# A decode attention kernel with less instruction code: register loops in place of written-out code on TensorE and VectorE

## The chip, the cores and the metric

One core of a Trainium2 chip runs the whole program. The metric is device time in microseconds (us), the median of several executions. Each comparison below ran both kernels on the same chip. "Fast" is the normal state of a run.

The engines are named as in the profile: PE is TensorE (PEld its weight loads), DVE VectorE, ACT ScalarE, POOL GpSimd, SP SyncE. Times without another word are microseconds from the start of the span.

## The reference, cut to what matters

Four tokens (B = 4, D = 512) pass through attention over a sliding window of a cache, and in parallel through a SwiGLU block.

```python
def reference(A_x, A_k_cache, A_v_cache, A_wq, A_wo, B_x, B_w_gate, B_w_up, B_w_down):
    x = A_x                                   # (4, 1, 512) bf16
    xn = _layernorm(x, axis=-1)               # eps 1e-5
    # attention: 32 query heads, 8 K/V heads, Dh 128, the last W = 4096 of 16384 positions
    q = (xn @ wq) ...                         # wq 512 x 4096
    scores = einsum("bhqd,bhkd->bhqk", q, k) * Dh ** -0.5
    o = softmax(scores) @ v
    att = o.reshape(B, 1, 4096) @ wo          # wo 4096 x 512
    ffn = (silu(xn @ w_gate) * (xn @ w_up)) @ w_down      # F = 1792
    return x + att + ffn
```

There are 32 pairs of a token and a K/V head. Each pair needs 1 MB of K and 1 MB of V, that is 67 million bytes of cache in all and 14 million of weights, 81.0 MB as the profile counts it.

## The kernel before

SyncE issues every load in one queue, in order. A load waits only where its buffer is still in use. Four slots each hold K and V.

```python
@block.sync
def _(eng):
    def load_k(i):
        if i >= NSL:                                   # NSL = 4
            eng.wait_ge(s_tr, NG * (i - NSL + 1))      # transposes of pair i-4 done
        eng.dma_start(KB[i % NSL][:], kv_ap(A_k_cache, i)).then_inc(d_k[i % NSL], 16)
    def load_v(i):
        if i == NSL - 1:
            eng.wait_ge(s_pv, 1)                       # the fourth V waits for the first P.V
        if i >= NSL:
            eng.wait_ge(s_pv, i - NSL + 2)
        eng.dma_start(VB[i % NSL][:], kv_ap(A_v_cache, i)).then_inc(d_v[i % NSL], 16)
    # W_Q half, X, W_Q half, K0, W_gate, W_up, W_down, V0, then K1 V1 ... K31 V31, then 8 loads of W_O
```

The slot of the fourth V holds zeros at first. P·V is the product of a pair's softmax weights P with its V. The first P·V is a dummy that multiplies them, so that the loop over pairs needs no special first pass. Therefore **no load after K3 is issued until TensorE has done its prologue and that first P·V**.

TensorE's prologue is written out, one matmul per line of the unrolled loop:

```python
for c in range(NC):                                    # Q: 4 x 32 matmuls
    if c % 2 == 0:
        eng.wait_ge(d_wq[c // 2], 16)
    for h in range(HQ):
        last = mm(q_ps[:, h * B:(h + 1) * B], WQ[:, c, h * Dh:(h + 1) * Dh], XnT[:, c, :], ...)
last.then_inc(s_q, 1)
for w, d, o in ((WG, d_wg, gate_ps), (WU, d_wu, up_ps)):   # gate, up: 14 x 4 matmuls each
    eng.wait_ge(d, 16)
    ...
# [cut: 14 down matmuls]
eng.wait_ge(s_nrm, 1)
with eng.Fori(0, HKV) as r:                            # the main loop was already a register loop
    for b in range(B):
        transposes(r, b)      # 32 transposes of K into PSUM, VectorE copies them out
        pv(r, b)              # P.V of the pair before
        scores(r, b)          # 32 matmuls, then exp on ScalarE
# [cut: permutation and W_O]
```

VectorE's code for the 32 pairs is written out, `for i in range(NPAIR): evac(i); ...; norm(i - 1)`.

The softmax here doesn't subtract the row's maximum and nothing guards it: scores larger than these inputs give would overflow.

## Time and profile before

| | before |
|---|---|
| time, median (lowest to highest) | 202.88 us (202.8 to 203.15), 3 runs |
| span of the profiled run | 201.1 us |
| bytes read | 81.01 MB at 403 GB/s over the span |
| PE busy | 80% |
| fourth V issued (= first P·V done) | 38.19 us |
| last W_O landing | 197.79 us |

The page of the kernel before: the slices are fortieths of the span (5.03 us), with busy tenths of PE and of the 16 DMA engines and the bandwidth, and then the chain that ended last, that is the waits followed back from the last instruction.

```profile
span 201.1 us, 7838 instructions
...
PE   0043779989989779797999889797979799795992
...
DMA  6999999999999999999999999999999999999980
GB/s 218 431 429 425 428 420 417 419 419 420 420 417 417 422 429 419 420 422 419 429 422 419 424 416 425 425 417 422 420 425 425 419 419 420 425 424 407 410 328 8
...
DMA 58%; PE 27%; DVE 6%; SPq 5%; issue 2%; ACT 0%; DVEq 0%
DMA kbuf<-in_A_k_cache_dram 39%; PE ps_kt L321 15%; DMA wu_sb<-in_B_w_up_dram 11%; DMA wo_sb<-in_A_wo_dram 9%; DVE kT L239 5%; PE ps_s L327 4%; PE ps_o L338 4%; SPq L174 3%; PE ps_m L311 2%; PE ps_m L303 2%; SPq L171 1%; PE ps_o L336 0%; PE ps_acc L352 0%; SPq L164 0%; SPq L180 0%
```

Reading it: DMA is at 9 from the second to the 38th of the 40 slices, at about 420 GB/s. PE is also nearly full, but the chain gives it 27% and DMA 58%. The queue of loads is never empty, so the stream of bytes decides the time.

TensorE's prologue and the issue of the loads that follow, from the timeline (start, duration, engine, line, operation, and in brackets the idle time before and what ended it):

```profile
13.47 3.57 PE L295 MATMUL ps_acc<-xnT,wq_sb 128*128 128x4 bf16 x128 [0.27 <-DVE xnT L227]
21.26 3.52 PE L303 MATMUL ps_m<-xnT,wg_sb 128*128 128x4 bf16 x56 [4.21 <-DMA wg_sb<-in_B_w_gate_dram]
25.39 3.52 PE L303 MATMUL ps_m<-xnT,wu_sb 128*128 128x4 bf16 x56 [0.61 <-DMA wu_sb<-in_B_w_up_dram]
```

```profile
38.19 0.33 SPq L171 DMA_DIRECT2D vbuf<-in_A_v_cache_dram  x1
38.56 0.43 SPq L164 DMA_DIRECT2D kbuf<-in_A_k_cache_dram  x1
```

128 Q matmuls take 3.57 us, and gate and up 3.52 us each. PE waits 4.21 us for W_gate in between. Written-out matmuls follow each other every 28 ns on average (3.57 us / 128); the weights arrive later than PE can use them. The up projection ends at 28.9 us and the fourth V is issued at 38.19 us, while earlier loads are still in flight until about 43 us.

Instruction fetches appear in the trace's DMA records as packets of their own. PE's are of 16384 B, at 19.1, 29.6, 42.4, 48.7, 55.3 and 194.6 us. The other engines' are of 8192 B, at 56.5, 117.5, 182.4 and 183.4 us. The records name a queue (q8 and q14) and not an engine; whose they are is inferred.

### The profile page before, as it was taken

The page shows a single profiled execution, that of the slowest core. Times are in us where ns is not written, and L with a number is a line of the kernel's source. Part 1 is how long each engine was busy: PE and PEld are TensorE (multiplying, and loading weights), DVE is VectorE, ACT ScalarE, POOL GpSimd, SP SyncE. Part 2 cuts the span into 40 slices and gives each one's busy share as a digit, 9 for nine tenths or more (in the row PEclk, how much of TensorE's full clock was granted, in tenths as well). Part 3 has the DMA queues.
Part 4 walks back from the last instruction along what each step waited for, and adds up shares of the span by engine and source line. Part 5 has one row for each costly group of instructions (what it writes and reads, how often), then busy time and mean ns, then how long its engine had stood idle before and what let it go on. Part 6 is the DMA issues. An engine that isn't in the chain of part 4 may idle for free.

```text
span 201.1 us, 7838 instructions
## 1 busy us (share of the span) xinstructions
PE 160.3 (80%) x3539; PEld 151.5 (75%) x3539; DVE 112.0 (56%) x277; ACT 11.9 (6%) x36; POOL 7.2 (4%) x29
## 2 busy tenths in 40 slices
PE   0043779989989779797999889797979799795992
PEld 0043662879989779797999889797979799795971
DVE  0340010686786666676666657576767657574640
ACT  2020000000000000000000000000000000000000
POOL 8600000000000000000000000000000000000000
PEclk9999999997999997969556957879797958788555
DMA  6999999999999999999999999999999999999980
GB/s 218 431 429 425 428 420 417 419 419 420 420 417 417 422 429 419 420 422 419 429 422 419 424 416 425 425 417 422 420 425 425 419 419 420 425 424 407 410 328 8
DMA packets 11138, 81.15 MB, mean 404 GB/s; under 512 B 1268, under 2 KB 1272, under 8 KB 2296
## 3 DMA queue, kind: packets, MB, share of 16 engines
q1 hardware_dynamic: 11112, 81.01, 97.1%
q8 instruction: 6, 0.10, 0.2%
q14 instruction: 4, 0.03, 0.0%
q10 hardware_dynamic: 16, 0.00, 0.0%
HBM read 81.01 MB, written 0.00 MB: 403 GB/s over the span
## 4 chain that ended last, share of the span: by engine, by line
DMA 58%; PE 27%; DVE 6%; SPq 5%; issue 2%; ACT 0%; DVEq 0%
DMA kbuf<-in_A_k_cache_dram 39%; PE ps_kt L321 15%; DMA wu_sb<-in_B_w_up_dram 11%; DMA wo_sb<-in_A_wo_dram 9%; DVE kT L239 5%; PE ps_s L327 4%; PE ps_o L338 4%; SPq L174 3%; PE ps_m L311 2%; PE ps_m L303 2%; SPq L171 1%; PE ps_o L336 0%; PE ps_acc L352 0%; SPq L164 0%; SPq L180 0%
## 5 line engine op out<-in xcount | busy, mean ns | idle before, releaser
L239 DVE COPY kT<-ps_kt 128x1024 bf16<-128x1024 bf16 x128 | 83.2, 687 | 47.7 <-PE ps_kt L321 47.3
L321 PE MATMUL ps_kt<-ident,kbuf 128*128 128x128 bf16 x1024 | 82.7, 255 | 10.7 <-DMA kbuf<-in_A_k_cache_dram 10.2
L321 PEld LDWEIGHTS ps_kt<-ident,kbuf 128*128 128x128 bf16 x1024 | 76.4, 117 | 12.9 <-issue 10.2
L327 PE MATMUL ps_s<-qC,kT 128*128 128x4 bf16 x1024 | 30.8, 165 | 6.5 <-DVE kT L239 6.4
L327 PEld LDWEIGHTS ps_s<-qC,kT 128*128 128x128 bf16 x1024 | 28.1, 97 | 8.2 <-DVE kT L239 8.1
L338 PE MATMUL ps_o<-p,vbuf 128*128 128x4 bf16 x1056 | 32.2, 165 | 0.0
L338 PEld LDWEIGHTS ps_o<-p,vbuf 128*128 128x128 bf16 x1056 | 31.5, 99 | 0.0
L202 ACT ACTIVATE p<-ps_s 128x128 bf16<-128x128 f32 x32 | 8.9, 278 | 152.9 <-PE ps_s L327 152.9
L287 PE MATMUL ps_m<-i,xn 4*128 4x4 f32 x4 | 0.6, 254 | 12.6 <-DVE xn L225 12.6
L287 PEld LDWEIGHTS ps_m<-i,xn 4*128 4x128 f32 x4 | 0.5, 207 | 12.6 <-issue 12.6
L245 DVE TENSOR_REDUCE den<-ps_o 128x4 f32<-128x128 f32 x32 | 9.1, 284 | 0.9 <-PE ps_o L338 0.8
L336 PE MATMUL ps_o<-p,ones 128*128 128x128 bf16 x33 | 8.3, 250 | 0.0
L247 DVE RECIPROCAL den<-den 128x4 f32<-128x4 f32 x32 | 5.7, 178 | 2.7 <-issue 0.4
L249 DVE TENSOR_TENSOR oT<-ps_o,den 128x4 bf16<-128x4 f32 x32 | 5.4, 168 | 2.7 <-issue 0.4
L303 PE MATMUL ps_m<-xnT,wg_sb 128*128 128x4 bf16 x56 | 3.5, 199 | 4.2 <-DMA wg_sb<-in_B_w_gate_dram 4.2
L303 PEld LDWEIGHTS ps_m<-xnT,wg_sb 128*128 128x128 bf16 x56 | 3.4, 159 | 4.3 <-DMA wg_sb<-in_B_w_gate_dram 4.3
L253 DVE TENSOR_SCALAR ex<-ex 128x56 f32<-128x56 f32 x1 | 0.2, 192 | 11.6 <-ACT ex L199 11.6
L311 PE MATMUL ps_m<-wd_sb,guT 128*4 128x512 bf16 x14 | 4.8, 518 | 1.7 <-DVE guT L259 1.7
L244 DVE COPY qC<-qT 128x4 bf16<-128x4 bf16 x28 | 4.6, 163 | 2.6 <-PE ps_o L338 2.3
L211 DVE TENSOR_REDUCE st_sum<-x_sb 4x1 f32<-4x512 bf16 x1 | 0.7, 673 | 8.3 <-DMA x_sb<-in_A_x_dram 8.3
L352 PE MATMUL ps_acc<-wo_sb,oP 128*4 128x128 bf16 x128 | 4.1, 306 | 1.3 <-DMA wo_sb<-in_A_wo_dram 1.3
L311 PEld LDWEIGHTS ps_m<-wd_sb,guT 128*4 128x4 bf16 x14 | 1.4, 107 | 4.7 <-issue 2.4
(44 smaller groups left out, 40.8 us busy)
## 6 DMA issues: line engine op xcount, KB each, us to landing
kbuf<-in_A_k_cache_dram SPq DMA_DIRECT2D x32, 1024.0 KB, 15.5
vbuf<-in_A_v_cache_dram SPq DMA_DIRECT2D x32, 1024.0 KB, 13.3
wq_sb<-in_A_wq_dram SPq DMA_DIRECT2D x2, 2048.0 KB, 9.5
wo_sb<-in_A_wo_dram SPq DMA_DIRECT2D x8, 512.0 KB, 18.3
wg_sb<-in_B_w_gate_dram SPq DMA_DIRECT2D x1, 1792.0 KB, 18.6
wu_sb<-in_B_w_up_dram SPq DMA_DIRECT2D x1, 1792.0 KB, 22.2
wd_sb<-in_B_w_down_dram SPq DMA_DIRECT2D x1, 1792.0 KB, 26.0
out_dram<-y_sb SPq DMA_DIRECT2D x2, 1.0 KB
```

What stands on the lines that cost most here:

```text
L174: eng.dma_start(WO[:, q], wo_ap[q]).then_inc(d_wo[q], 16)
L202: eng.activation(P[j % 2][:], ps_S[:, 0:NT * REP].rearrange("p (t h) -> p t h", h=REP), ACT.Exp, scale=SCALE).then_inc(s_p, 1)
L239: eng.tensor_copy(KT[i % 2][:, a:a + 8, :], kt_ps[g % 4]).then_inc(s_ev, 1)
L245: eng.tensor_reduce(den[:], den_ps.rearrange("p (t h) -> p h t", h=REP), AX.X, ALU.add)
L247: eng.reciprocal(den[:], den[:])
L249: eng.tensor_tensor(OT[:, j // B, :, j % B], O_ps, den[:], ALU.mult).then_inc(s_nrm, 1)
L303: last = mm(o[:, t * B:(t + 1) * B], w[:].rearrange("p c (m t) -> p c t m", t=NF)[:, c, t, :], XnT[:, c, :], start=(w is WG and t == 0 and ...
L311: last = mm(down_ps, guT[:, t, :], WD[:, t, :], start=(t == 0), stop=(t == NF - 1))
L321: last = eng.transpose(kt_ps[n % 4][:, k, :], KB[b][:, 8 * g + k, :], ident[:])
L327: last = mm(ps_S[:, REP * t:REP * (t + 1)], KT[b % 2][:, t, :], QC[:, b])
L336: mm(den_ps, ones[:], P[p % 2][:].rearrange("p t h -> p (t h)"))
L338: last = mm(O_ps, VB[p][:, t, :], P[p % 2][:, t, :], start=(t == 0), stop=(t == NT - 1))
```

## The change

The intent is less instruction code, and so fewer instruction fetches on the DMA engines that carry the cache (in the trace of before, with a fetch of 16384 B at 19.1 us, 15 of W_gate's 16 landings come by 19.84 us and one at 21.21 us). TensorE's Q, gate and up become loops over registers (`Fori`: the engine itself counts in a register and branches back), VectorE's 32 pairs become a loop, there are 74 loads in place of 78, W_O uses two column tiles of 256 with two output DMAs, and the layernorm is shortened, with X loaded by ScalarE's queue. The score matmuls read Q at a register address in place of a copy by VectorE. The core of the diff (cuts marked with `...`):

```diff
-            for c in range(NC):
-                if c % 2 == 0:
-                    eng.wait_ge(d_wq[c // 2], 16)
-                for h in range(HQ):
-                    last = mm(q_ps[:, h * B:(h + 1) * B], WQ[:, c, h * Dh:(h + 1) * Dh], XnT[:, c, :], ...
+            zero = VB[:, (NSL - 1) * KVN:(NSL - 1) * KVN + 128]
+            mm(q_ps, zero, zero, start=True, stop=False, skip_group_check=True)
+            mm(ps_m[:, 0:128], zero, zero, start=True, stop=False, skip_group_check=True)
+            for g in range(2):
+                eng.wait_ge(d_wq[g], 16)
+                with eng.Fori(0, 8) as j:
+                    o = q_ps[:, ds((j & 3) * 32, 32)]
+                    w = WQf[:, ds(j * 1024 + 8192 * g, 1024)]
+                    x = XTf[:, ds((j & 4) + 8 * g, 4)]
+                    for k in range(8):
+                        last = mm(o[:, 4 * k:4 * k + 4], w[:, 128 * k:128 * k + 128], x, start=False, ...
...
             for w, d, o in ((WG, d_wg, 0), (WU, d_wu, 64)):
                 eng.wait_ge(d, 16)
-                for t in range(NF):
-                    for c in range(NC):
+                with eng.Fori(0, NF // 2) as t:
+                    oo = ps_m[:, ds(t * 8 + o, 8)]
+                    ww = w[:].rearrange("p c (m t) -> p c t m", t=NF)[:, :, ds(t * 2, 2), :]
+                    for k in range(2):
+                        for c in range(NC):
...
-            for i in range(NPAIR):
+            with eng.Fori(0, NPAIR) as i:
                 evac(i)
-                if i > 0:
-                    norm(i - 1)
+                norm(i)
...
-            eng.tensor_scalar(xc[:], X[:], st_mean[:, 0:1], None, ALU.subtract)
-            eng.tensor_tensor(xsq[:], xc[:], xc[:], ALU.mult)
-            eng.tensor_reduce(st_sum[:], xsq[:], AX.X, ALU.add)
+            eng.tensor_scalar(xc[:], X[:], float(D), st_sum[:, 0:1], ALU.mult, ALU.subtract).then_inc(s_xc, 1)
+            # ScalarE: eng.activation(xsq[:], xc[:], ACT.Square, accum_out=st_sum[:, 0:1])
...
-                    for n in range(NC):
-                        last = mm(ps_acc[32 * n:32 * n + B, 0:128], OP[:, e, q, :],
-                                  WO[:, q, e, 128 * n:128 * n + 128], start=False,
+                    for n in range(2):
+                        last = mm(ps_acc[64 * n:64 * n + B, 0:256], OP[:, e, q, :],
+                                  WO[:, q, e, 256 * n:256 * n + 256], start=False,
```

More of the change, by code (lines that the diff above doesn't have):

```diff
@@ L36, in bass_parallel_sum__sliding_block_cached__swiglu_ffn__decode_kernel @@
     NG = 4
+    KVN = NT * Dh
+    PN = NT * REP
     SCALE = float(Dh) ** -0.5
@@ L45, in bass_parallel_sum__sliding_block_cached__swiglu_ffn__decode_kernel @@
     st_sum = sb("st_sum", [B, 1], FP32)
-    st_mean = sb("st_mean", [B, 1], FP32)
     st_var = sb("st_var", [B, 1], FP32)
@@ L56, in bass_parallel_sum__sliding_block_cached__swiglu_ffn__decode_kernel @@
     QT = sb("qT", [128, HKV, B, REP], BF16)
-    QC = sb("qC", [128, B, REP], BF16)
-    KB = [sb("kbuf%d" % s, [128, NT, Dh], BF16) for s in range(NSL)]
-    VB = [sb("vbuf%d" % s, [128, NT, Dh], BF16) for s in range(NSL)]
-    KT = [sb("kT%d" % s, [128, NT, 128], BF16) for s in range(2)]
-    P = [sb("p%d" % s, [128, NT, REP], BF16) for s in range(2)]
+    KB = sb("kbuf", [128, NSL * NT * Dh], BF16)
+    VB = sb("vbuf", [128, NSL * NT * Dh], BF16)
+    KT = sb("kT", [128, 2 * NT * 128], BF16)
+    P = sb("p", [128, 2 * NT * REP], BF16)
     den = sb("den", [128, REP], FP32)
-    OT = sb("oT", [128, HKV, REP, B], BF16)
+    OT = sb("oT", [128, 1 + NPAIR, REP], BF16)
     OP = sb("oP", [128, REP, HKV, B], BF16)
@@ L72, in bass_parallel_sum__sliding_block_cached__swiglu_ffn__decode_kernel @@
     y0 = sb("y0", [B, D], FP32)
-    I4w = sb("i4w", [B, 32], FP32)
-    y = sb("y_sb", [128, 128], BF16)
+    I4w = sb("i4w", [B, 64], FP32)
+    y = sb("y_sb", [128, 256], BF16)
     ps = nc.alloc_psum_tensor
@@ L87, in bass_parallel_sum__sliding_block_cached__swiglu_ffn__decode_kernel @@
     up_ps = ps_m[:, 64:64 + NF * B]
-    perm_ps = ps_m[:].rearrange("p (e k h b) -> p h e k b", e=REP, k=HKV, h=REP)
+    perm_ps = ps_m[:].rearrange("p (e k b h) -> p h e k b", e=REP, k=HKV, h=REP)
     q_ps = ps_acc[:, 0:HQ * B]
-    down_ps = ps_m[0:B, :]
+    down_ps = ps_acc[0:B, :]
     xT_ps = ps_m[:, 128:128 + NC * B]
@@ L100, in bass_parallel_sum__sliding_block_cached__swiglu_ffn__decode_kernel @@
     d_out = sem("d_out")
-    d_wo = [sem("d_wo%d" % q) for q in range(HKV)]
+    WO_CUTS = (0, 3, 6, 7, 8)
+    d_wo = [sem("d_wo%d" % q) for q in range(len(WO_CUTS) - 1)]
+    s_xc = sem("s_xc")
+    s_ss = sem("s_ss")
     d_k = [sem("d_k%d" % s) for s in range(NSL)]
@@ L127, in bass_parallel_sum__sliding_block_cached__swiglu_ffn__decode_kernel @@
     x_ap = A_x.rearrange("b s d -> (b s) d")
-    out_ap = out.rearrange("b s (n c) -> n (b s) c", n=NC)
+    out_ap = out.rearrange("b s (n c) -> n (b s) c", n=2)
     wq_ap = A_wq.rearrange("(p c) n -> p c n", c=NC)
@@ L132, in bass_parallel_sum__sliding_block_cached__swiglu_ffn__decode_kernel @@
     wd_ap = B_w_down.rearrange("(p t) n -> p t n", t=NF)
-    wo_ap = A_wo.rearrange("(k p e) n -> k p e n", k=HKV, e=REP)
+    wo_ap = A_wo.rearrange("(k p e) n -> p k (e n)", k=HKV, e=REP)
+    ds = bass.ds
     def kv_ap(cache, i):
@@ L152, in _ @@
             eng.tensor_copy(I4w[:, 0:B], I4[:])
-            for e in range(REP):
-                for h in range(REP):
-                    eng.tensor_copy(sel[:, e, h, :], ident[:].rearrange("p (m e) -> p e m", e=REP)[:, e, :])
-            eng.memset(P[1][:], 0.0)
-            eng.memset(VB[NSL - 1][:], 0.0).then_inc(s_const, 1)
+            for h in range(REP):
+                eng.tensor_copy(sel[:, :, h, :], ident[:].rearrange("p (m e) -> p e m", e=REP))
+            eng.memset(P[:, PN:2 * PN], 1.0)
+            eng.memset(VB[:, (NSL - 1) * KVN:], 0.0).then_inc(s_const, 1)
         @block.sync
@@ L163, in load_k @@
                     eng.wait_ge(s_tr, NG * (i - NSL + 1))
-                eng.dma_start(KB[i % NSL][:], kv_ap(A_k_cache, i)).then_inc(d_k[i % NSL], 16)
+                eng.dma_start(KB[:, i % NSL * KVN:(i % NSL + 1) * KVN].rearrange("p (t d) -> p t d", t=NT), kv_ap(A_k_cache, i)).then_inc(d_k[i % NSL], 16)
             def load_v(i):
@@ L170, in load_v @@
                     eng.wait_ge(s_pv, i - NSL + 2)
-                eng.dma_start(VB[i % NSL][:], kv_ap(A_v_cache, i)).then_inc(d_v[i % NSL], 16)
-            def load_wo(q):
-                eng.dma_start(WO[:, q], wo_ap[q]).then_inc(d_wo[q], 16)
+                eng.dma_start(VB[:, i % NSL * KVN:(i % NSL + 1) * KVN].rearrange("p (t d) -> p t d", t=NT), kv_ap(A_v_cache, i)).then_inc(d_v[i % NSL], 16)
             eng.dma_start(WQ[:, 0:2], wq_ap[:, 0:2]).then_inc(d_wq[0], 16)
-            eng.dma_start(X[:], x_ap).then_inc(d_x, 16)
             eng.dma_start(WQ[:, 2:4], wq_ap[:, 2:4]).then_inc(d_wq[1], 16)
@@ L186, in _ @@
                 load_v(i)
-            for q in range(HKV):
-                load_wo(q)
+            for n in range(len(d_wo)):
+                a, b = WO_CUTS[n], WO_CUTS[n + 1]
+                eng.dma_start(WO[:, a:b].rearrange("p k e n -> p k (e n)"), wo_ap[:, a:b]).then_inc(d_wo[n], 16)
             eng.wait_ge(s_y, 1)
-            for n in range(0, NC, 2):
-                eng.dma_start(out_ap[n], y[32 * n:32 * n + B, :]).then_inc(d_out, 16)
-            eng.wait_ge(d_out, 16 * NC)
+            eng.dma_start(out_ap[0], y[0:B, :]).then_inc(d_out, 16)
+            eng.wait_ge(d_out, 32)
         @block.scalar
         def _(eng):
+            eng.dma_start(X[:], x_ap).then_inc(d_x, 16)
+            eng.wait_ge(s_xc, 1)
+            eng.activation(xsq[:], xc[:], ACT.Square, accum_out=st_sum[:, 0:1]).then_inc(s_ss, 1)
             eng.wait_ge(s_var, 1)
@@ L201, in _ @@
                 eng.wait_ge(s_sc, j + 1)
-                eng.activation(P[j % 2][:], ps_S[:, 0:NT * REP].rearrange("p (t h) -> p t h", h=REP),
-                               ACT.Exp, scale=SCALE).then_inc(s_p, 1)
+                eng.activation(P[:, j % 2 * PN:(j % 2 + 1) * PN], ps_S[:, 0:PN], ACT.Exp, scale=SCALE).then_inc(s_p, 1)
             eng.wait_ge(s_y, 1)
-            for n in range(1, NC, 2):
-                eng.dma_start(out_ap[n], y[32 * n:32 * n + B, :]).then_inc(d_out, 16)
+            eng.dma_start(out_ap[1], y[64:64 + B, :]).then_inc(d_out, 16)
         @block.vector
@@ L212, in _ @@
             eng.drain()
-            eng.tensor_scalar(st_mean[:], st_sum[:], 1.0 / D, None, ALU.mult)
-            eng.drain()
-            eng.tensor_scalar(xc[:], X[:], st_mean[:, 0:1], None, ALU.subtract)
-            eng.drain()
-            eng.tensor_tensor(xsq[:], xc[:], xc[:], ALU.mult)
-            eng.drain()
-            eng.tensor_reduce(st_sum[:], xsq[:], AX.X, ALU.add)
-            eng.drain()
-            eng.tensor_scalar(st_var[:], st_sum[:], 1.0 / D, EPS, ALU.mult, ALU.add).then_inc(s_var, 1)
+            eng.tensor_scalar(xc[:], X[:], float(D), st_sum[:, 0:1], ALU.mult, ALU.subtract).then_inc(s_xc, 1)
+            eng.wait_ge(s_ss, 1)
+            eng.tensor_scalar(st_var[:], st_sum[:], 1.0 / D, EPS * D * D, ALU.mult, ALU.add).then_inc(s_var, 1)
             eng.wait_ge(s_std, 1)
@@ L228, in _, with norm @@
             eng.wait_ge(s_q, 1)
-            eng.tensor_copy(QT[:], q_ps.rearrange("p (k h b) -> p k b h", k=HKV, b=B))
-            eng.drain()
-            eng.tensor_copy(QC[:], QT[:, 0]).then_inc(s_nrm, 1)
+            eng.tensor_copy(QT[:], q_ps.rearrange("p (k h b) -> p k b h", k=HKV, b=B)).then_inc(s_nrm, 1)
             eng.engine_nop().then_inc(s_ev, 3)
             def evac(i):
-                for g in range(NG * i, NG * i + NG):
-                    eng.wait_ge(s_tr, g + 1)
-                    a = 8 * (g % NG)
-                    eng.tensor_copy(KT[i % 2][:, a:a + 8, :], kt_ps[g % 4]).then_inc(s_ev, 1)
-            def norm(j):
-                eng.wait_ge(s_pv, j + 2)
-                if j + B < NPAIR:
-                    eng.tensor_copy(QC[:, j % B], QT[:, j // B + 1, j % B])
+                for g in range(NG):
+                    eng.wait_ge(s_tr, i * NG + (g + 1))
+                    eng.tensor_copy(KT[:, ds((i & 1) * KVN + 1024 * g, 1024)],
+                                    kt_ps[g].rearrange("p a b -> p (a b)")).then_inc(s_ev, 1)
+            def norm(j1):
+                eng.wait_ge(s_pv, j1 + 1)
                 eng.tensor_reduce(den[:], den_ps.rearrange("p (t h) -> p h t", h=REP), AX.X, ALU.add)
@@ L248, in norm @@
                 eng.drain()
-                eng.tensor_tensor(OT[:, j // B, :, j % B], O_ps, den[:], ALU.mult).then_inc(s_nrm, 1)
+                eng.tensor_tensor(OT[:].rearrange("p j h -> p (j h)")[:, ds(j1 * REP, REP)], O_ps, den[:],
+                                  ALU.mult).then_inc(s_nrm, 1)
             def ffn():
@@ L267, in _ @@
             ffn()
-            for i in range(NPAIR):
+            eng.wait_ge(s_dn, 1)
+            eng.tensor_add(y0[:], X[:], down_ps).then_inc(s_y0, 1)
+            with eng.Fori(0, NPAIR) as i:
                 evac(i)
-                if i == 0:
-                    eng.wait_ge(s_dn, 1)
-                    eng.tensor_add(y0[:], X[:], down_ps).then_inc(s_y0, 1)
-                if i > 0:
-                    norm(i - 1)
+                norm(i)
             perm_copy(1, 0, HKV - 1)
-            norm(NPAIR - 1)
+            norm(NPAIR)
             perm_copy(2, HKV - 1, HKV)
             eng.wait_ge(s_acc, 1)
-            eng.tensor_copy(y[:], ps_acc[:, 0:128]).then_inc(s_y, 1)
+            eng.tensor_copy(y[:], ps_acc[:, 0:256]).then_inc(s_y, 1)
         @block.tensor
@@ L290, in _ @@
             eng.wait_ge(s_xnT, 1)
-            for c in range(NC):
-                if c % 2 == 0:
-                    eng.wait_ge(d_wq[c // 2], 16)
-                for h in range(HQ):
-                    last = mm(q_ps[:, h * B:(h + 1) * B], WQ[:, c, h * Dh:(h + 1) * Dh], XnT[:, c, :],
-                              start=(c == 0 and h == 0), stop=(c == NC - 1), skip_group_check=True)
-            last.then_inc(s_q, 1)
-            for w, d, o in ((WG, d_wg, gate_ps), (WU, d_wu, up_ps)):
-                eng.wait_ge(d, 16)
-                for t in range(NF):
-                    for c in range(NC):
-                        last = mm(o[:, t * B:(t + 1) * B],
-                                  w[:].rearrange("p c (m t) -> p c t m", t=NF)[:, c, t, :], XnT[:, c, :],
-                                  start=(w is WG and t == 0 and c == 0), stop=(c == NC - 1),
-                                  skip_group_check=True)
@@ L307, in _ @@
-            last.then_inc(s_gu, 1)
+            zero = VB[:, (NSL - 1) * KVN:(NSL - 1) * KVN + 128]
+            mm(q_ps, zero, zero, start=True, stop=False, skip_group_check=True)
+            mm(ps_m[:, 0:128], zero, zero, start=True, stop=False, skip_group_check=True)
+            WQf = WQ[:].rearrange("p c n -> p (c n)")
+            XTf = XnT[:].rearrange("p c b -> p (c b)")
+            for g in range(2):
[5 more added lines that the diff above has]
+                    for k in range(8):
+                        last = mm(o[:, 4 * k:4 * k + 4], w[:, 128 * k:128 * k + 128], x, start=False, stop=True, skip_group_check=True)
@@ new lines, in _ @@
+            mm(q_ps[:, 0:4], zero, zero[:, 0:4], start=False, stop=True, skip_group_check=True).then_inc(s_q, 1)
+            for w, d, o in ((WG, d_wg, 0), (WU, d_wu, 64)):
+                eng.wait_ge(d, 16)
+                with eng.Fori(0, NF // 2) as t:
[3 more added lines that the diff above has]
+                        for c in range(NC):
+                            mm(oo[:, 4 * k:4 * k + 4], ww[:, c, k, :], XnT[:, c, :], start=False, stop=True, skip_group_check=True)
@@ L308, in _ @@
+            mm(ps_m[:, 0:4], zero, zero[:, 0:4], start=False, stop=True, skip_group_check=True).then_inc(s_gu, 1)
             eng.wait_ge(s_guT, 1)
@@ L317, in transposes @@
                 for g in range(NG):
-                    n = NG * b + g
-                    eng.wait_ge(s_ev, r * (NG * B) + n)
+                    eng.wait_ge(s_ev, r * (NG * B) + (NG * b + g))
                     for k in range(8):
-                        last = eng.transpose(kt_ps[n % 4][:, k, :], KB[b][:, 8 * g + k, :], ident[:])
+                        a = b * KVN + 128 * (8 * g + k)
+                        last = eng.transpose(kt_ps[g][:, k, :], KB[:, a:a + 128], ident[:])
                     last.then_inc(s_tr, 1)
@@ L325, in scores @@
                 eng.wait_ge(s_ev, r * (NG * B) + (NG * (b + 1) + 3))
+                q = QT[:].rearrange("p k b h -> p (k b h)")[:, ds(r * (B * REP) + b * REP, REP)]
                 for t in range(NT):
-                    last = mm(ps_S[:, REP * t:REP * (t + 1)], KT[b % 2][:, t, :], QC[:, b])
+                    a = b % 2 * KVN + 128 * t
+                    last = mm(ps_S[:, REP * t:REP * (t + 1)], KT[:, a:a + 128], q)
                 last.then_inc(s_sc, 1)
             def pv(r, b):
-                p = (b - 1) % B
-                eng.wait_ge(d_v[p], r * 16 + (16 if b else 0))
+                j = (b - 1) % B
+                eng.wait_ge(d_v[j], r * 16 + (16 if b else 0))
                 eng.wait_ge(s_p, r * B + b)
-                eng.wait_ge(s_nrm, r * B + b)
-                mm(den_ps, ones[:], P[p % 2][:].rearrange("p t h -> p (t h)"))
+                eng.wait_ge(s_nrm, r * B + (b + 1))
+                p = j % 2 * PN
+                mm(den_ps, ones[:], P[:, p:p + PN])
                 for t in range(NT):
-                    last = mm(O_ps, VB[p][:, t, :], P[p % 2][:, t, :], start=(t == 0), stop=(t == NT - 1))
+                    a = j * KVN + 128 * t
+                    last = mm(O_ps, VB[:, a:a + 128], P[:, p + REP * t:p + REP * (t + 1)],
+                              start=(t == 0), stop=(t == NT - 1))
                 last.then_inc(s_pv, 1)
@@ L344, in permute @@
                     last = mm(ps_m[:, o + a * REP * B:o + b * REP * B], sel[:, e].rearrange("p h m -> p (h m)"),
-                              OT[:, a:b].rearrange("p k h b -> p (k h b)"))
+                              OT[:, 1 + B * a:1 + B * b].rearrange("p j h -> p (j h)"))
                 last.then_inc(s_pm, 1)
             def wo(q):
-                eng.wait_ge(d_wo[q], 16)
+                if q in WO_CUTS:
+                    eng.wait_ge(d_wo[WO_CUTS.index(q)], 16)
                 for e in range(REP):
-                    for n in range(NC):
-                        last = mm(ps_acc[32 * n:32 * n + B, 0:128], OP[:, e, q, :],
-                                  WO[:, q, e, 128 * n:128 * n + 128], start=False,
+                    for n in range(2):
+                        last = mm(ps_acc[64 * n:64 * n + B, 0:256], OP[:, e, q, :],
+                                  WO[:, q, e, 256 * n:256 * n + 256], start=False,
                                   stop=(q == HKV - 1 and e == REP - 1), skip_group_check=True)
@@ L364, in _ @@
             permute(0, HKV - 1)
-            for n in range(NC):
-                mm(ps_acc[32 * n:32 * n + 32, 0:128], I4w[:], y0[:, 128 * n:128 * n + 128],
+            for n in range(2):
+                mm(ps_acc[64 * n:64 * n + 64, 0:256], I4w[:], y0[:, 256 * n:256 * n + 256],
                    start=True, stop=False, skip_group_check=True)
@@ L370, in _ @@
             wo(0)
-            eng.wait_ge(s_nrm, NPAIR + 1)
+            eng.wait_ge(s_nrm, NPAIR + 2)
             permute(HKV - 1, HKV)
```

## The prediction

> **What bounds the kernel now.** The DMA stream. The page's slices show DMA busy 0.9 or more from the second slice to the last but one, at about 420 GB/s; 81.0 MB pass. K loads take 15.5 us from issue to landing (DMA view): the queue is never short. PE is busy 80%, but the chain of waits is 58% DMA. The last W_O load lands at 197.8 us; 3.3 us follow.
>
> **What the change aims at.** Instruction fetches use the same DMA engines ([...]five packets of 16384 B between 19 and 55 us, one at 194.6, and four of 8192 B at 56.5, 117.5, 182.4, 183.4 for others). Each makes one engine late for good: of W_gate's 16 landings 15 come at 19.5 to 19.8 us, one at 21.2. The last load's landings spread from 194.8 to 197.8. Without fetches up to 2.7 us would go. PE's program falls from 1680 to about 1200 instructions, VectorE's from 358 to 62: no VectorE fetch, about three PE fetches in the stream. If none hit the same engine, the stream ends 1.3 us earlier; W_O and output give 0.3 us. Alone that is 201.3 us. An earlier X and a shorter layernorm gain nothing.
>
> **What it costs.** The Q and gate/up loops need a register instruction before each of 240 matmuls, two or three more per iteration, and 30 loop ends. In the trace of before, PE's sequencer instructions follow each other at 96 ns (register ALU) and 102 to 106 ns (fused register operation); an ALU with 16 static PE instructions takes 112 ns, so static matmuls are almost free there; a taken branch takes 289 ns. Estimate: a Q iteration 1.4 to 1.6 us (16 of them), a gate/up iteration 1.25 to 1.4 us (14): 40 to 45 us in place of 3.6 + 3.5 + 3.5 us. Q can start at 8.3 us (the first W_Q half lands at 8.2), so up ends at 49 to 54 us, not 28.9. That is critical: the fourth V load is held until the first P·V (38.19 us before, 9.2 us after up). What was issued earlier has landed by 43 us, so it must be issued by about 41. First P·V at 59 to 64 us leaves the engines idle for 17 to 22 us. Less 1.6: 218 to 224 us.
>
> Main loop: VectorE saves a 163 ns Q copy per pair and gains about 0.3 us of register work; the PE and VectorE cycle is 4.0 us (chain of waits) against 5.0 us of DMA per pair: hidden, unless dynamic score matmuls issue slower than their 30 ns.
>
> **Doubt.** If register instructions between matmuls overlap better than these samples show (under 0.8 us an iteration), the stream never dries and 201 to 203 us results. Median 217 us, range 200.8 to 226; faster by over 2% 0.02, within 2% 0.36, slower by over 2% 0.62.
>
> **What would show it.** Right: up matmuls ending near 50 us; a DMA gap from about 43 us in the slices; fourth V issued near 60 us; Q and gate matmuls over 100 ns apart; fewer 16384 B packets, no VectorE fetch after the start, final landings spread under 2 us. Wrong: up ends before 32 us and no gap; or score groups longer than 1 us and PE paces the pairs.

## More of the kernel before

The layernorm's centring, and the end of the kernel:

```profile
L215 DVE TENSOR_SCALAR xc<-x_sb,st_mean x1: 475/475/475, 9.3 to 9.3; 4x512 f32<-4x512 bf16 x1
```

```profile
196.59 0.60 PE L352 MATMUL ps_acc<-wo_sb,oP 128*4 128x128 bf16 x16 [0.54 <-DMA wo_sb<-in_A_wo_dram]
...
197.93 0.60 PE L352 MATMUL ps_acc<-wo_sb,oP 128*4 128x128 bf16 x16 [0.74 <-DMA wo_sb<-in_A_wo_dram]
198.57 0.29 DVE L279 CAST y_sb<-ps_acc 128x128 bf16<-128x128 f32 x1 [4.00 <-PE ps_acc L352]
```

The centring of a 4x512 tile takes 475 ns. At the end PE waits for the last W_O load, then needs 0.60 us for its row block of 512 rows.

## The result, and the profile after

The changed kernel takes 238.11 us (237.36 to 239.05, 4 runs); the kernel before takes 202.93 us on the same chip. The ratio is 1.1734, with a 95% interval of 1.169 to 1.1778. A ratio here is the mean time of one kernel's fast runs over the mean time of the other's fast runs of the same rounds, so it is not quite the ratio of the quoted medians. The change is slower by 35.2 us, far outside the predicted range.

| | before | after |
|---|---|---|
| span | 201.1 us | 235.2 us |
| Q matmuls | 13.47 to 17.04 | 11.66 to 44.08 (the next matmul at 44.15) |
| up ends | 28.9 | 66.1 (with the matmul that closes its loop) |
| fourth V issued | 38.19 | 75.07 |
| stretch without a load packet | none | 42.93 to 76.02 |
| pairs, first to last exp | 39.5 to 190.7 (mean 4.87 us) | 76.7 to 224.2 (mean 4.76 us) |
| last W_O landing | 197.79 | 232.22 |
| PE's wait for K, total | 10.2 us | 1.1 us |

The same lines of the page after (a slice is 5.88 us):

```profile
span 235.2 us, 8501 instructions
...
PE   0166655777768998899888979889998988989895
...
DMA  7999999200001999999999999999999999999992
GB/s 265 424 433 429 410 421 421 96 0 0 0 0 17 372 398 417 341 418 424 418 419 424 421 419 421 418 422 418 424 422 419 422 415 422 418 424 422 410 409 116
...
PE 55%; DMA 22%; issue 11%; DVE 7%; SPq 3%; ACT 1%; DVEq 0%
PE ps_kt L318 25%; DMA kbuf<-in_A_k_cache_dram 13%; PE ps_acc L293 9%; PE ps_s L326 8%; DMA wo_sb<-in_A_wo_dram 8%; PE ps_m L303 7%; DVE kT L230 4%; PE ps_o L339 4%; SPq L188 2%; PE ps_acc L308 2%; DVE xc L214 2%; DMA x_sb<-in_A_x_dram 1%; ACT L199 1%; PE ps_o L336 0%; SPq L174 0%
```

The count of instructions is of those executed: with loops there is less code, but the register and branch instructions are executed again and again, so it rises from 7838 to 8501. Slices 9 to 12 have no traffic at all, with a remnant on either side. PE is busy in them, but these are register-addressed matmuls with a long step. The same views of the prologue and of the loads:

```profile
11.66 1.27 PE L293 MATMUL ps_acc<-xnT,wq_sb 128*128 x8 [0.25 <-issue]
13.69 1.30 PE L293 MATMUL ps_acc<-xnT,wq_sb 128*128 x8 [0.75 <-issue]
```

```profile
44.55 1.13 PE L303 MATMUL ps_m<-xnT,wg_sb 128*128 128x4 bf16 x8 [0.21 <-issue]
46.10 1.15 PE L303 MATMUL ps_m<-xnT,wg_sb 128*128 128x4 bf16 x8 [0.42 <-issue]
```

```profile
67.80 4.50 PE L308 MATMUL ps_acc<-wd_sb,guT 128*4 128x512 bf16 x14 [1.69 <-DVE guT L251]
...
74.09 0.95 PE L339 MATMUL ps_o<-p,vbuf 128*128 128x4 bf16 x32
```

```profile
75.07 0.33 SPq L174 DMA_DIRECT2D vbuf<-in_A_v_cache_dram  x1
75.44 0.54 SPq L167 DMA_DIRECT2D kbuf<-in_A_k_cache_dram  x1
80.37 0.33 SPq L174 DMA_DIRECT2D vbuf<-in_A_v_cache_dram  x1
```

Each group of eight matmuls is an iteration. A Q iteration starts every 2.03 us: eight matmuls in 1.3 us, then 0.75 us of idle time that the profile calls "issue" (nothing is waited for; in the records of PE's sequencer a branch, busy 215 to 225 ns where it is taken, and six or seven register instructions lie between the last matmul's weight load and the next iteration's first). A gate iteration starts every 1.55 us. After up come the down matmuls (L308), and then the first P·V (L339), which ends at 75.04 us. The fourth V and the fifth K, which used to go out at 38 us, go out at 75 us, 32 us after the last load in flight has landed.

The layernorm and the memset of GpSimd that now runs beside it, and the end of the kernel:

```profile
2.16 0.97 POOL L158 COPY sel<-ident 128x128 bf16<-128x128 bf16 x4
...
2.94 4.06 DVE L214 TENSOR_SCALAR xc<-x_sb,st_sum 4x512 f32<-4x512 bf16 x1
3.07 0.19 POOL L159 MEMSET p<- 128x128 bf16 x1
...
3.21 3.50 POOL L160 MEMSET vbuf<- 128x4096 bf16 x1
...
7.77 1.28 ACT L199 ACT_TABLE_LOAD   x1
```

```profile
229.75 3.21 PE L355 MATMUL ps_acc<-wo_sb,oP 128*4 128x256 bf16 x40 [0.18 <-DMA wo_sb<-in_A_wo_dram]
...
233.00 0.42 DVE L269 CAST y_sb<-ps_acc 128x256 bf16<-128x256 f32 x1 [4.48 <-PE ps_acc L355]
```

The centring takes 4.06 us in place of 0.475 us and ends just after the memset (6.71 us). At the end 40 W_O matmuls in 3.21 us run until the last landing and past it.

The first reading is therefore: the first P·V comes 37 us later, 33 of them leave the DMA engines without work, and the end moves by 35 us. The main loop is not slower: pairs are 4.76 us apart against 4.87 us.

### The profile page after: what moved, and what is told of

Its sections match the earlier page's. It is cut to its first block, busy times and chain, and to the rows that moved or that the text cites. A ratio compares the mean times of both kernels' runs of the same rounds, so it can differ in the third digit from the quotient of the medians.

```text
span 235.2 us, 8501 instructions
## 1 busy us (share of the span) xinstructions
PE 189.9 (81%) x3475; PEld 170.4 (72%) x3475; DVE 112.6 (48%) x248; ACT 13.9 (6%) x39; POOL 5.8 (2%) x17
## 4 chain that ended last, share of the span: by engine, by line
PE 55%; DMA 22%; issue 11%; DVE 7%; SPq 3%; ACT 1%; DVEq 0%
PE ps_kt L318 25%; DMA kbuf<-in_A_k_cache_dram 13%; PE ps_acc L293 9%; PE ps_s L326 8%; DMA wo_sb<-in_A_wo_dram 8%; PE ps_m L303 7%; DVE kT L230 4%; PE ps_o L339 4%; SPq L188 2%; PE ps_acc L308 2%; DVE xc L214 2%; DMA x_sb<-in_A_x_dram 1%; ACT L199 1%; PE ps_o L336 0%; SPq L174 0%
## 5 line engine op out<-in xcount | busy, mean ns | idle before, releaser
L230 DVE COPY kT<-ps_kt 128x1024 bf16 x128 | 83.4, 687 | 39.7 <-PE ps_kt L318 38.2
L326 PE MATMUL ps_s<-qT,kT 128*128 x1024 | 30.7, 165 | 11.4 <-DVE kT L230 10.4
L326 PEld LDWEIGHTS ps_s<-qT,kT 128*128 128x128 bf16 x1024 | 28.0, 97 | 14.1 <-issue 12.7
L339 PE MATMUL ps_o<-p,vbuf 128*128 128x4 bf16 x1056 | 32.3, 165 | 0.0
L339 PEld LDWEIGHTS ps_o<-p,vbuf 128*128 128x128 bf16 x1056 | 31.7, 99 | 0.0
L293 PE MATMUL ps_acc<-xnT,wq_sb 128*128 x128 | 20.5, 184 | 12.2 <-issue 12.1
L293 PEld LDWEIGHTS ps_acc<-xnT,wq_sb 128*128 x128 | 13.4, 105 | 19.5 <-issue 13.6
L303 PE MATMUL ps_m<-xnT,wu_sb 128*128 128x4 bf16 x56 | 8.0, 218 | 2.9 <-issue 2.9
L303 PE MATMUL ps_m<-xnT,wg_sb 128*128 128x4 bf16 x56 | 8.0, 215 | 2.6 <-issue 2.6
L303 PEld LDWEIGHTS ps_m<-xnT,wu_sb 128*128 x56 | 7.2, 138 | 3.7 <-issue 3.5
L303 PEld LDWEIGHTS ps_m<-xnT,wg_sb 128*128 x56 | 7.3, 138 | 3.3 <-issue 3.0
L240 DVE TENSOR_TENSOR oT<-ps_o,den 128x4 f32 (+1 forms) x33 | 5.4, 162 | 5.3 <-issue 5.2
## 6 DMA issues: line engine op xcount, KB each, us to landing
wo_sb<-in_A_wo_dram SPq DMA_DIRECT2D x2, 1536.0 KB, 19.6
```

The costliest lines, as they stand in the source:

```text
L230: eng.tensor_copy(KT[:, ds((i & 1) * KVN + 1024 * g, 1024)], kt_ps[g].rearrange("p a b -> p (a b)")).then_inc(s_ev, 1)
L240: eng.tensor_tensor(OT[:].rearrange("p j h -> p (j h)")[:, ds(j1 * REP, REP)], O_ps, den[:], ALU.mult).then_inc(s_nrm, 1)
L293: last = mm(o[:, 4 * k:4 * k + 4], w[:, 128 * k:128 * k + 128], x, start=False, stop=True, skip_group_check=True)
L303: mm(oo[:, 4 * k:4 * k + 4], ww[:, c, k, :], XnT[:, c, :], start=False, stop=True, skip_group_check=True)
L326: last = mm(ps_S[:, REP * t:REP * (t + 1)], KT[:, a:a + 128], q)
L339: last = mm(O_ps, VB[:, a:a + 128], P[:, p + REP * t:p + REP * (t + 1)], start=(t == 0), stop=(t == NT - 1))
```

## The experiments

**Theory.** The register loops in TensorE's prologue delay the first P·V, and the queue runs dry between about 43 us and the issue of the fourth V. The earlier loads have landed by 43 us and a load's first packet follows its issue by about 1 us (75.07 and 76.02 us in the trace of after), so the fourth V must be issued by about 41 to 42 us; every microsecond after that is lost. **Rivals.** VectorE's register loop or the register-addressed score operand slows the pairs; or the two wide W_O tiles cost the tail. Each experiment is an edit of the changed kernel unless it says otherwise. All twelve gave a correct result.

### 1. Q, gate and up written out (a1_unroll_all)

```diff
-                with eng.Fori(0, 8) as j:
-                    o = q_ps[:, ds((j & 3) * 32, 32)]      # and w, x likewise
+                for j in range(8):
+                    o = q_ps[:, (j & 3) * 32:(j & 3) * 32 + 32]
-                with eng.Fori(0, NF // 2) as t:
+                for t in range(NF // 2):
```

> The changed kernel with TensorE's Q and gate/up loops written out, everything else of the change kept (VectorE's loop, the score matmuls' register address, 74 loads, two column tiles). Theory (the register loops before attention cost it all, by emptying the load queue): up ends near 29 us, the fourth V is issued near 38 us, no gap in the slices, 201 to 202.5 us. Rival (VectorE's loop or the register address of the score matmuls slows the main loop): 210 us or more with no early gap, and pairs paced by TensorE in the chain of waits. Last W_O landing: spread under 2 us with no 8192 B fetch in the stream, against 3.0 us before; worth about 1 us.

Measured: 202.36 us (202.19 to 203.06, 6 runs), ratio 0.9984 (0.9971 to 0.9997). The fourth V goes out in time:

```profile
39.02 0.33 SPq L174 DMA_DIRECT2D vbuf<-in_A_v_cache_dram  x1
```

Up ends at 29.0 us, and there is no gap. The VectorE loop, the register-addressed scores, the wide W_O tiles and the shorter layernorm are all still in this kernel, so none of them costs the 35 us. The theory holds and both rivals fall as a cause of the 35 us. The last W_O landings spread from 195.31 to 197.17 us, under 2 us as expected, but that is worth 0.6 us in the last landing and not about 1 us.

### 2 and 3. Only Q, or only gate and up, written out (a2_unroll_q, a3_unroll_gu)

The edit is one half of experiment 1 each.

> Only the Q loops written out, gate/up still loops. If each loop costs what its own stretch in the trace shows (32.5 us for Q, 10.8 for each of gate and up) and the loads wait only for the first P.V: Q ends near 17 us, gate starts at 19.8 when its weights land, up ends near 41.5, first P.V near 50.5, gap about 9 us, total about 212 us. If the loss is not the prologue's length but the main loop: about 235.

> Only gate/up written out, Q still two loops. Q ends near 44.2 us as now, gate and up take 7 us together, first P.V near 60.5, gap about 18.5 us, total about 223.5 us. If the costs of the loops did not add up: away from 223 by over 3 us.

Measured, one run each: 216.5 us with Q written out, 223.44 us with gate and up written out. The second was 0.1 us from its expectation. The first was 4.5 us above: the fourth V went out at 52.48 us, 2 us later than expected, and the last W_O load landed at 210.19 us, 4.3 us before the end of the span of 214.5 us, because 40 W_O matmuls after the third-last landing took 4.43 us. That already hinted that PE, and not only the loads, can set the end (experiments 10 to 12).

The two together show that both loops count and that the delays add up:

| kernel | fourth V issued | stretch without packets | time over before |
|---|---|---|---|
| a1_unroll_all | 39.02 us | none | -0.55 us |
| a2_unroll_q | 52.48 us | 9.3 us | 13.6 us |
| a3_unroll_gu | 61.73 us | 19.9 us | 20.5 us |
| a4_memset_later (below) | 72.86 us | 31.0 us | 32.8 us |
| the change | 75.07 us | 33.1 us | 35.2 us |

### 4. The memset after the centring (a4_memset_later)

The prediction let Q start at 8.3 us; it started at 11.66 us. The theory is a collision of the centring with GpSimd's memset of 128x4096.

```diff
             eng.memset(P[:, PN:2 * PN], 1.0)
+            eng.wait_ge(s_xc, 1)
             eng.memset(VB[:, (NSL - 1) * KVN:], 0.0).then_inc(s_const, 1)
```

> The changed kernel with GpSimd's 128x4096 memset held until VectorE has written xc. Theory (the memset, now at the same time as xc, stretches that 4x512 operation from 0.47 to 4.06 us and so the start of Q): xc takes about 0.5 us, Q starts 2.5 to 3.3 us earlier, the total falls by as much, to about 235 us. Rival (xc is slow for another reason, as the fresh arrival of x): xc still 4 us, no change of the total.

Measured: 235.73 us (234.89 to 237.2, 4 runs), ratio 1.1641 (1.1613 to 1.1669), 2.4 us faster than the change by the medians, 1.9 us by the ratios. Its timeline:

```profile
2.94 0.60 DVE L215 TENSOR_SCALAR xc<-x_sb,st_sum 4x512 f32<-4x512 bf16 x1
...
3.60 3.51 POOL L161 MEMSET vbuf<- 128x4096 bf16 x1 [0.34 <-DVE xc L215]
...
4.33 0.14 DVE L217 TENSOR_SCALAR st_var<-st_sum 4x1 f32<-4x1 f32 x1 [0.79 <-ACT xsq L198]
...
6.07 1.31 DVE L221 TENSOR_SCALAR xn<-xc,st_rstd 4x512 f32<-4x512 f32 x1
...
9.06 1.28 PE L294 MATMUL ps_acc<-xnT,wq_sb 128*128 x8 [0.25 <-issue]
```

The centring takes 0.60 us, Q starts 2.6 us earlier. Now the next 4x512 instruction, the scaling that writes xn, meets the memset and takes 1.31 us (0.47 us in the traces of before and after, where it does not meet it), until 0.27 us after the memset's end. The 4x1 instruction at 4.33 us, in the midst of the memset, takes 0.14 us, as in the trace of before after its memset. So the two 4x512 instructions that met it were held (4.06 us against 0.475 us, and 1.31 us against 0.47 us) and the 4x1 one was not; what holds them was not shown, no record names it. The centring of the change is recorded from 2.94 us, before the long memset (3.21 us), while the last of GpSimd's four copies into sel runs, from 2.85 to 3.13 us; GpSimd's instructions follow each other without a gap until 6.71 us. In this run the centring ended 0.28 us after the short memset of p (3.07 us), in the change 0.29 us after the long one. So VectorE was held over several GpSimd instructions in a row.

### 5. The fourth V not held (a5_no_hold)

If the loads alone set the end, taking away the held load should give the time of one load.

```diff
-                if i == NSL - 1:
-                    eng.wait_ge(s_pv, 1)
-            zero = VB[:, (NSL - 1) * KVN:(NSL - 1) * KVN + 128]
+            zero = zt[:]                      # a zeroed tile of its own; the memset goes to KT
             eng.wait_ge(s_nrm, 1)
+            eng.wait_ge(d_v[NSL - 1], 16)
```

> The changed kernel, but the fourth V load is issued at once: the zeros that the first P.V and the start matmuls read lie elsewhere (GpSimd still writes as many bytes at the same time), and TensorE waits for that V before the attention loop. Theory (the cost is the time for which the load queue is empty): the queue holds one 1 MB load more, so the gap begins 2.5 us later, near 45.4 us, while the first P.V stays near 75 us; the total falls 2.5 us, to about 235.6 us. Rival (the cost is TensorE's own time and the loads don't matter): no change, 238 us.

Measured: 238.24 us (236.93 to 239.28, 4 runs), ratio 1.1737 (1.1693 to 1.1781): no gain. The gap is there from 45.32 to 76.64 us, so it opens 2.4 us later than in the change, by the time of one load. Then only the fifth K could go out, at 75.67 us; the next V waited for the next P·V, until 80.80 us. The held load was one of the many that wait on the same pairs: the gap only moved to the next of them. The expectation failed, and with it the simple form of the theory, that the loads alone decide the end.

### 6. One register address per Q matmul (a6_q_two_reg)

A Q matmul of the change computes two addresses (weights and output), since the register expression of its input is the same for the group. Here the loop runs over the contraction blocks, so that only the weight address changes from matmul to matmul.

```diff
-                with eng.Fori(0, 8) as j:
-                    o = q_ps[:, ds((j & 3) * 32, 32)]
-                    w = WQf[:, ds(j * 1024 + 8192 * g, 1024)]
-                    x = XTf[:, ds((j & 4) + 8 * g, 4)]
-                    for k in range(8):
+                with eng.Fori(0, 2) as c:
+                    w = WQf[:, ds(c * 4096 + 8192 * g, 4096)]
+                    x = XTf[:, ds(c * 4 + 8 * g, 4)]
+                    for h in range(HQ):
```

> The changed kernel with Q's loop turned: each iteration is one c with all 32 heads written out, so only the weight address changes from matmul to matmul (the output address is fixed, x's is set once per iteration). Theory (each matmul costs the sequencer its register operation plus about 78 ns, and the register operation grows with the number of addresses it works out: 74 ns busy and 152 ns apart with two addresses, 46 and 124 in gate/up with one): 124 ns per matmul, Q about 19 us instead of 32.5, total about 224.5 us. Rival (a matmul with any register address costs the same): 152 ns per matmul, Q about 22.5 us for the 12 fewer loop ends, total about 228.

Measured, one run: 224.83 us.

```profile
11.35 4.18 PE L292 MATMUL ps_acc<-xnT,wq_sb 128*128 x32
16.03 4.10 PE L292 MATMUL ps_acc<-xnT,wq_sb 128*128 x32 [0.50 <-issue]
```

An iteration of 32 matmuls takes 4.18 us, 131 ns a matmul, and the idle time at the loop's end is paid 4 times in place of 16. Q takes 18.3 us in place of 32.5 us. The cost is per register address and per iteration, as the theory has it: in the trace's records of PE's sequencer the fused register instruction is busy 74 ns where it forms two addresses (matmuls 152 ns apart) and 46 ns where it forms one (124 ns apart in gate and up). The step is in both cases that time plus 78 ns.

### 7. W_O back to four column tiles, on top of experiment 1 (c1_four_tiles)

```diff
-                    for n in range(2):
-                        last = mm(ps_acc[64 * n:64 * n + B, 0:256], OP[:, e, q, :],
+                    for n in range(NC):
+                        last = mm(ps_acc[32 * n:32 * n + B, 0:128], OP[:, e, q, :],
```

(and the four output DMAs of before)

> a1_unroll_all (Q and gate/up written out) with W_O back in four column tiles of 128 and four output DMAs; W_O still in four loads. Theory ([...]8 matmuls of 256 took 1.02 us against 16 of 128 in 0.60 us, and at the low clock W_O then paces the end): the W_O matmuls end 0.6 to 0.7 us after the last landing with idle time ahead of it, total equal to a1_unroll_all or up to 0.3 us less, 202.1 to 202.4 us. Rival (two output DMAs save more than the tiles cost): 0.3 us slower than a1_unroll_all, 202.7.

Measured: 202.32 us (202.29 to 202.38, 5 runs), ratio 0.997 (0.9956 to 0.9983), against 0.9984 (0.9971 to 0.9997) for experiment 1. The intervals overlap, so the tile width is worth nothing measurable while the loads end last, although a row block of W_O takes 1.02 us in two tiles (8 matmuls, in the trace of after) and 0.60 us in four (16 matmuls), both at a granted clock of 0.50 (the share of TensorE's full clock that the profile shows). In both kernels the last W_O matmul ends 0.7 us after the last landing. In four tiles PE waits 0.73 us for that landing; in the two tiles of experiment 1 its last 56 matmuls run without a pause from 192.83 to 197.91 us and reach the last row block about when it lands.

### 8. The VectorE loop written out, on top of experiment 1 (d1_unroll_dve)

```diff
-            with eng.Fori(0, NPAIR) as i:
+            for i in range(NPAIR):
```

> a1_unroll_all with VectorE's loop over pairs written out too. If the loop's register work is what took TensorE's slack (its waits for K: 10.2 us in the kernel before, 0.8 us in a1_unroll_all): these waits come back to 8 us or more and a pair takes 4.0 instead of 4.26 us at full clock. If VectorE's instruction fetches are what the change saved: 8192 B fetches are back in the stream and the last landing moves back by up to 0.6 us: 202.4 to 203.0 us. Rival (the loop costs something on the critical path): faster than a1_unroll_all.

Measured: 203.17 us (203.02 to 203.29, 5 runs), ratio 1.001 (0.9996 to 1.0024). Three fetches of 8192 B are back in the stream, at 61.4, 128.4 and 196.4 us, and the last W_O landing is at 198.42 us against 197.17 us. A pair of PE and VectorE work takes 4.1 us at full clock in place of 4.3 us. PE's waits for K tell what became of these 0.2 us, in the order before, after, experiment 1, this one:

```profile
PE ps_kt L321 <- DMA kbuf<-in_A_k_cache_dram: 10.2, 15, 1.8
```

```profile
PE ps_kt L318 <- DMA kbuf<-in_A_k_cache_dram: 1.1, 3, 0.5
```

```profile
PE ps_kt L318 <- DMA kbuf<-in_A_k_cache_dram: 0.8, 2, 0.5
```

```profile
PE ps_kt L318 <- DMA kbuf<-in_A_k_cache_dram: 6.1, 10, 0.9
```

The columns are the waiter, what it waited for, total us, times, longest. With VectorE's loop in the kernel PE hardly waits for K (0.8 us and 1.1 us); without it PE waits 6.1 us. The register work of VectorE used up PE's slack and did no harm. Two sizes were missed: the waits for K were expected to be 8 us or more, and the landing at most 0.6 us later, where it was 1.25 us. Of these, 0.95 us arise in the last load alone: the load before it landed at 196.20 us against 195.91 us, and the fetch at 196.4 us lies between the two. The loop is the part of the change that pays, by the fewer fetches: 0.8 us by the medians, 0.5 us by the ratios, whose intervals (on two chips) just touch.

### 9. More instruction fetches in the kernel before (f1_more_fetches)

The claim that a fetch costs time for good was only argued until here. This is the kernel before, with 768 no-operations on GpSimd, which else has nothing to do there.

```diff
             eng.memset(VB[NSL - 1][:], 0.0).then_inc(s_const, 1)
+            eng.wait_ge(s_pv, 12)
+            for _ in range(768):
+                eng.engine_nop()
```

> The kernel before, with 768 idle instructions on GpSimd from the 12th P.V on (about 80 us); it does no work there otherwise. Theory (an instruction fetch makes the DMA engine that carries it late for good, and the last load waits for the latest engine): about six more 8192 B fetches in the stream; if they fall on one engine, 0.5 to 0.8 us each, the last landing is 1 to 3 us later and the kernel takes 204 to 206 us; if each falls on another engine the last landing moves by at most 0.8 us. Rival (fetches cost the stream nothing that lasts): landings and time unchanged, 202.9 us.

Measured: 203.78 us (203.67 to 203.98, 4 runs), ratio 1.0043 (1.0028 to 1.0057). The DMA queues of the instruction fetches, before and then here:

```profile
q14 instruction: 4, 0.03, 0.0%
```

```profile
q14 instruction: 10, 0.08, 0.1%
```

The page counts six more packets; in the trace they lie between 93 and 118 us, while the no-operations run. The landings of the last W_O load by the 16 engines spread from 194.79 to 198.58 us, against 194.77 to 197.79 us: the earliest engines end as before, the last one ends 0.8 us later, and the kernel 0.85 us, 80 us after the fetches. The rival, that the stream makes up for it, falls. No run has the no-operations without their fetches; that they slow anything by themselves is not excluded by a run, but GpSimd has no other work there.

### 10 to 12. Which chain ends last after the gap (a7_wo_early, a8_early_fast, a9_fast_only)

Experiment 5 gave nothing. Either only PE's time counts after the prologue, or PE's work and the loads are two chains of about equal length. First the loads of W_O, 4 MB and 10 us of the stream, go into the gap, where the engines are idle:

```diff
             for i in range(1, NPAIR):
                 load_k(i)
+                if i == NSL - 1:
+                    # the four W_O loads, taken away from the end
                 load_v(i)
```

> The changed kernel with the four W_O loads (4 MB, 10 us of the stream) issued before the held fourth V, so that they fill part of the gap; nothing else. a5_no_hold has shown that a shorter gap need not be a shorter kernel: its gap only moved behind the next release. Refined theory (the K and V loads come two per pair, when a P.V frees their slots, so the first P.V at 75 us sets when the last V lands, about 222 us, and TensorE with it; W_O is no longer in the way at the end): gap 10 us shorter, but the total falls only by what W_O took at the end, and TensorE is close behind: the last pair ends near 227.5, then 3 to 5 us of W_O matmuls: 2 to 4 us less, about 235 us. Naive theory (time lost = time in which the queue is empty): 10 us less, about 228. Rival (TensorE's time alone): no change.

Measured: 238.18 us (236.9 to 238.93, 4 runs), ratio 1.173 (1.1689 to 1.1771): nothing gained. The expectation failed. The W_O loads landed by 53.6 us, and the last V by 224.1 us in place of W_O's last landing at 232.2 us, and yet the kernel ended no earlier. Its last exp was at 226.5 us and then 56 W_O matmuls took 5.44 us. In this profile the down matmuls took longer than in that of the change and its fourth V went out 1.4 us later, at 76.47 us; the medians of four runs show that this does not hide a gain.

So both were shortened together, and the other half alone: VectorE's loop written out and four W_O tiles, with W_O early (a8_early_fast) and with W_O at the end (a9_fast_only).

> A two by two test of what the tail of the changed kernel waits for. This is the changed kernel with the W_O loads issued into the gap (as in the run where that alone changed nothing, 238.18 us) and besides with the pairs made shorter (VectorE's loop written out, 4.1 us in place of 4.3 us a pair at full clock) and W_O in four column tiles (0.60 in place of 1.02 us a row block). Theory, that after the prologue the loads and the work of TensorE and VectorE are two chains of about equal length, so that shortening either alone gives nothing: shortening both gives 2 to 5 us, a median of 233 to 236 us. Rival, that only the prologue's delay counts and nothing after it: 238 us again.

> The other cell of the two by two test: the changed kernel with the pairs and W_O made shorter and the W_O loads left at the end. Theory: the last W_O landing, near 232 us as in the changed kernel, sets the end; the four column tiles after it save 0.3 us at most, the three written-out fetches of VectorE cost up to 1 us: 237.5 to 239 us, no gain. Rival, that the pairs alone were the longer chain: 2 us or more faster than the changed kernel.

| | W_O loads at the end | W_O loads in the gap |
|---|---|---|
| VectorE loop, two W_O tiles | 238.11 us, ratio 1.1734 | 238.18 us, ratio 1.173 |
| written out, four W_O tiles | 239.28 us (238.52 to 239.9), ratio 1.1776 (1.1753 to 1.18) | 235.44 us (234.77 to 236.05), ratio 1.1599 (1.1569 to 1.1629) |

Neither alone gains; both together gain 2.7 us, within what the theory of two equal chains expected. The W_O matmuls at the end of a7_wo_early and of a8_early_fast:

```profile
229.35 5.44 PE L356 MATMUL ps_acc<-wo_sb,oP 128*4 128x256 bf16 x56
```

```profile
228.01 3.16 PE L358 MATMUL ps_acc<-wo_sb,oP 128*4 128x128 bf16 x112
```

Of the 3.2 us between the spans of these two (237.0 and 233.8 us), 2.3 us are the W_O matmuls (5.44 against 3.16 us for the same seven row blocks) and 1.1 us an earlier last exp (225.4 against 226.5 us). Part of my expectation was wrong in its reason: the pairs did not become shorter on average, they are 4.77 us apart in a8_early_fast and 4.76 us in the change, so nearly all of the gain is W_O's tile width; this is read from two traces, and no run separates the two halves. In a9_fast_only, 0.3 us above its expected range, the end was again a landing. PE's fetch of 16384 B at 232.7 us and VectorE's of 8192 B at 231.4 us came back with the written-out code, and the last landing was at 234.93 us, with the engine before it at 233.27 us:

```profile
231.50 1.45 PE L357 MATMUL ps_acc<-wo_sb,oP 128*4 128x128 bf16 x48 [1.99 <-DMA wo_sb<-in_A_wo_dram]
...
233.73 0.60 PE L357 MATMUL ps_acc<-wo_sb,oP 128*4 128x128 bf16 x16 [0.78 <-DMA wo_sb<-in_A_wo_dram]
...
235.07 0.60 PE L357 MATMUL ps_acc<-wo_sb,oP 128*4 128x128 bf16 x16 [0.74 <-DMA wo_sb<-in_A_wo_dram]
```

What stays open is what paces the pairs in the middle of the stream of the change. They are 4.75 to 4.80 us apart in all the changed kernels but d1_unroll_dve (4.85 us), whether a pair of PE work takes 4.1 or 4.3 us at full clock, and a load pair takes about 5.0 us; PE's granted clock changes between 1.00 and 0.50 during it. No run separates the two there. The trace of the change shows this much: from 105 us on the DMA engines are always busy and K lands every 4.99 us, while the time from a pair's K landing to its exp shrinks from 9.8 us (pair 8, counted from 0) to 4.6 us (pair 28). So PE is not held to the pace of the loads there (it waits 1.1 us for K in all); it uses up a lead, and the two chains come together only near the end.

## Why the prediction was wrong

The mechanism was the predicted one, at about twice the size (35.2 us; the slow branch of the prediction, 218 to 224 us, had 15 to 21 us), and the prediction gave it too little room. Point by point:

1. **The bound of the kernel before** was right. The stream of loads decides; experiments 1 and 9 move the end with its last landing.
2. **The mechanism** was right: up ends late, the fourth V is held, and a gap opens at 43 us. Written out again, the loops cost nothing (experiment 1).
3. **The step that failed is the cost of an iteration**: "a Q iteration 1.4 to 1.6 us (16 of them), a gate/up iteration 1.25 to 1.4 us (14): 40 to 45 us". Measured: 2.01 to 2.14 us and 1.55 us, together 54.4 us. The estimate took 96 to 106 ns for a register instruction from the few that the trace of before had, in the main loop, and treated the matmul after it as free. In the change a fused register instruction with two addresses and its matmul need 152 ns, with one address 124 ns, and 0.75 and 0.40 us per iteration go to the loop's own arithmetic and branch.
4. **The second term that failed is Q's start**: "Q can start at 8.3 us (the first W_Q half lands at 8.2)", and the earlier X and the shorter layernorm were taken to cost nothing. It started at 11.66 us. X landed early as meant, and just that moved the centring under GpSimd's memset (4.06 us); the new order of activation tables (loads at 1.33, 7.77 and 9.28 us) put one of 1.28 us (7.77 us) into the layernorm's chain besides. The trace of before has two loads, also of 1.28 us (0.74 and 11.74 us) and neither in that chain, so the cost of one could have been counted; that one comes between Square and Sqrt only the trace of the change shows. Nothing but the load itself shows there: ScalarE's instruction before it ends at 7.75 us, and the one after it starts at 9.06 us.
5. **What follows the gap**: "Less 1.6" for fewer fetches and the shorter tail did not come. After the gap the slices run at 372, 398, 417 and 341 GB/s in place of 420, worth 2.1 us (152 GB/s missing in sum, over 420, times 5.88 us); the loads go out only as pairs end (75.07, 80.37, 85.43 us). And the saving on loads buys nothing while PE's chain is as long (experiments 5 and 10 to 12).
6. **The fetches** were right in kind. The changed kernel has four PE fetches and no 8192 B packet in the stream, and its last landings spread over 1.5 us (230.68 to 232.22) in place of 3.0 us; since its queue ran empty at 43 us, that spread is no clean test. Nor does a run measure the predicted 1.3 us like for like, since that counted fewer PE fetches too. Experiment 1, with PE's six fetches and without the four of 8192 B, gained 0.55 us by the medians and 0.3 us by the ratio (0.6 us in the last landing); experiment 8 gives 0.5 to 0.8 us for VectorE's part alone.
7. **The main loop.** The pair cycle at full clock went from 4.0 to 4.3 us, the 0.3 us of register work that the prediction counted (the Q copy that it took off does not show), and in experiment 1 it is hidden, as predicted. After the gap it is not, because PE's chain is then as long as the loads' (experiments 10 to 12). The score matmuls are as fast as static ones (32 in 0.95 us): all 32 read Q at the same register address, and the trace shows one fused register instruction before the 32 and none between them.

The sum of the prediction's slow branch and what the runs showed:

| term | predicted | measured |
|---|---|---|
| Q starts | 8.3 us | 11.66 us |
| Q, 16 iterations | 22.4 to 25.6 us | 32.5 us |
| gate and up, 14 iterations | 17.5 to 19.6 us | 21.6 us |
| end of up to the fourth V | 9.2 us | 9.0 us |
| fourth V issued | 59 to 64 us | 75.07 us |
| time | 218 to 224 us | 238.11 us |

The 13.6 us between the middle of the predicted issue and the measured one, the 1.6 us that did not come and the 2.1 us of the restart make 17.3 us; from the middle of that branch, 221 us, to the median it is 17.1 us. The point of 217 us lay still lower because it was drawn towards a branch of 201 to 203 us, in which the loops would overlap and cost nothing, and to which 0.36 was given. The trace of before gave no ground for that: its samples, with everything static free, already gave the 40 to 45 us.

## What to carry to other kernels

The loops over registers saved instruction fetches (10 within the span before, 4 after), but each matmul for which a new address is formed in a register costs its sequencer time in series (here 124 to 152 ns against 28 ns; the 32 score matmuls of a pair share one register address, pay once and take 0.95 us), so put it only where the engine waits for something anyway: here the loop over VectorE's pairs gains 0.5 to 0.8 us, and those in TensorE's prologue lose 35 us. The version with Q, gate and up written out and VectorE's loop kept is the best one that was run (202.32 us with four W_O tiles, ratio 0.997), and it beats both kernels, the one before by only 0.3%. Before a prologue is lengthened, look for the load that is held until its end, and add up when the queue runs dry; and when something is taken off the stream, ask first whether the work that consumes it is just as long.
